# Linear attention and a gated feed-forward block on one core: the operand sums of a Strassen product and the loads of v are moved in the program

## The chip, the cores and the metric

The kernel runs on one core of a Trainium2 chip. The metric is the time of one execution on the device in microseconds (us), the median of several runs. A profiled execution gives the rows that are shown here. The engines are TensorE (PE, with its weight loads as PEld), VectorE (DVE), ScalarE (ACT) and GpSimd (POOL); SyncE (SP) issues most of the DMAs. Each engine works through its own queue in the order of the program; semaphores make it wait for others.

## What is computed

```python
q, k, v: (8, 8, 576, 64)       # batch, heads, sequence, head size; float32
w_gate, w_val: (512, 1536);  w_out: (1536, 512)

q_s = softmax of q over the head size
k_s = softmax of k over the sequence
kv  = einsum('bhsd,bhse->bhde', k_s, v)
x   = einsum('bhsd,bhde->bhse', q_s, kv)   as (4608, 512)
g   = x @ w_gate
out = (gelu(g) * (x @ w_val)) @ w_out      # (4608, 512), gelu with erf
```

## The kernel before

**Blocks.** Tokens are worked on in nine blocks of 512, in the order 0 to 6, 8, 7. Blocks 0 to 7 hold 512 of the 576 tokens of a batch each; block 8 holds the remaining 64 of every batch (called "rem" in the code, `xtr` for its x). `b` is the block, `B` is 8.

**A block's feed-forward part.** The hidden size of 1536 is cut into twelve tiles of 128 (`fi` 0 to 11, "tile 0" to "tile 11" in the text). For each tile TensorE makes `psg` and `psv` by four matmuls of 512 columns each (`mm_gv`, L424). ACT takes GELU of `psg` to `gl` (L429), and VectorE multiplies `psv`, a constant and `gl` to `ht` in float16 (L430; the text calls this the gate). So a gate sets `psv`'s bank free.

**PSUM banks.** Six banks go round in a ring (`ring`, `big`): each new tile takes the bank at the head, and its tag goes to the end at once, or, with `hold=True`, when `let_go` is called. Two more banks (`ps_att`) serve the attention part. A matmul into a bank waits until the bank's former content has been read.

**The output product.** In block 0, h @ w_out is made directly (`mm_out`). In all other blocks `out_strassen` makes it with seven half-size products in place of eight (Strassen and Winograd): h is cut into four quarters (by hidden half and token half), w_out into four, and `product(i, ...)` runs 12 matmuls of 256 columns (L545). For it, VectorE makes four sums of quarters of w_out once (`sum_w`, the tiles `tw`, L514, in block 1), and in each block four sums of quarters of h (`sum_h`, L531): sum 1 and 2 give `sh` 1 and 2, sum 3 overwrites a quarter of `ht`, sum 4 gives `s4`. A sum over hidden tiles j0 to j1 needs the gates of tiles j0 to j1 and 6 + j0 to 6 + j1, so it can be made in parts while the tiles are being finished. Products 1, 2 and 4 read plain `ht`; 5 and 6 read `sh` 1 and 2, 3 reads `s4`, 7 the overwritten quarter. Three banks are held: `psa` (products 1, then 6, 7 and 4 added to it), `psc` (5, then 3 added) and `psb` (2). `snap` copies a bank between two products for the output (`sn`, L571), `add` adds a bank to such a copy and writes `yo` (L577). Products run in the order 1, 5, 6, 3, 7, 2, 4.

**The attention part rides along.** `plan` is a table written by hand: `at(b, FI, i, ...)` puts work behind tile i of block b, `at(b, NS, i, ...)` behind certain products of `out_strassen`; `ride` issues it. For the next batches there are: loads of q, k and v (`load_batch`, issued by SP); exp on ACT (L178); the sums for the softmax of q on VectorE (`norm_sum`, L196, L198) and the multiplication by them on POOL (`norm_mul`, L215); a transpose by DMA (`unit_td`, L343); the cast of v to float16 on POOL (`cast_v`, L154); k's product with v and its normalization (`unit_kv4`, L300); and x by `unit_x4` (L387), with copies to `xt` on ACT and VectorE. There is one buffer for the loaded v (`vt`), and there are two each for q and k.

**Start.** Before block 0, two k sums (`ksum_mm`, `pks`) are made by matmul and inverted on VectorE (`ksum_rec`, `rck`, L270); then k's product with v for four pairs of heads (`kv0_mm`, `pskv`, L278), with the casts of v, x of batch 0, and the first tiles' matmuls.

These lines say where the sums and v's casts stand:

```python
    SUMS = {7: (0, 2), 9: (2, 4), 10: (4, 5)}     # behind these tiles, sums 1 to 4 of these hidden tiles
    for i in range(4):
        at(1, FI, 3 + i, L(sum_w, i + 1))
            at(b, FI, 0, L(load_batch, b + 2))
            at(b, FI, NFI - 1, L(exp, "q", b + 2), L(exp, "k", b + 2), L(cast_v, b + 2, 0, H))
            sum_h(NO - 1, NO, (1, 2))             # after tile 11; sums 3 and 4 of it in out_strassen
```

Of the kernel before, what the change touches and what calls it, by code (L numbers as in the profile page):

```python
# [18 lines left out]
def kernel(  # L19
# [15 lines left out]
    P = 128  # L35
# [39 lines left out]
    def let_go(t):  # L75
        ring.append(held.pop(id(t))[1])
# [183 lines left out]
    def ksum_mm(g):  # L260
        st[("pks", g)] = big([P, 2], f32, "pks")
        for j in range(2):
            hp = 2 * g + j
            for n in range(NC):
                nc.tensor.matmul(st[("pks", g)][:, j:j + 1], ek_b[0][:, n, hp * P:(hp + 1) * P],
                                 ones, start=(n == 0), stop=(n == NC - 1))

    def ksum_rec(g):
        st[("rck0", g)] = att.tile([P, 2], f32, name="rck0", tag="rck0")
        nc.vector.reciprocal(out=st[("rck0", g)], in_=st[("pks", g)])  # L270

    def kv0_mm(hp):
# [259 lines left out]

    SUMS = {7: (0, 2), 9: (2, 4), 10: (4, 5)}

# [14 lines left out]
    def out_strassen(b, last):  # L549
# [25 lines left out]
        def add(nm, sn, half, col):  # L575
            for t, src in parts(nm):
                nc.vector.scalar_tensor_tensor(  # L577
                    out=yo[half][:, t, c[col]], in0=src, scalar=1.0 / _H_SCALE,
                    in1=sn[:, t], op0=ALU.mult, op1=ALU.add)
# [13 lines left out]
        for x in tiles_["c"]:  # L593
            let_go(x)
        product(7, ps["a"], False)
# [115 lines left out]
    def at(b, kind, i, *fns):  # L711
# [30 lines left out]
    at(1, FI, 11, L(load_batch, 3), L(exp, "k", 2, 4, 8), L(exp, "q", 3), L(exp, "k", 3), L(exp_rem0), L(cast_v, 3, 0, H))  # L742
    for i in range(4):
        at(1, FI, 3 + i, L(sum_w, i + 1))
    at(1, FI, 6, make_s)
    at(1, NS, 2, L(unit_kv4, 2))
# [3 lines left out]
    for b in range(2, B):  # L750
        if b + 2 < B:
            at(b, FI, 0, L(load_batch, b + 2))
            at(b, FI, NFI - 1, L(exp, "q", b + 2), L(exp, "k", b + 2), L(cast_v, b + 2, 0, H))
        if b + 1 < B:
            n = b + 1
            for hp in range(HP):
                at(b, FI, hp, L(norm_sum, n, hp), L(norm_mul, n, hp, "pool"))
            at(b, FI, 4, L(unit_td, n))
            if n == 3:
                at(b, FI, 5, L(unit_kv4, n))  # L760
            at(b, NS, 4, L(unit_x4, n, ("act", "dve"), 0 if n == 4 else None))
            if n + 1 < B:
                at(b, NS, 4, L(unit_kv4, n + 1, n == 4))
# [6 lines left out]
    for b in order:  # L770
# [9 lines left out]
        for fi in range(fi0, NFI):  # L780
            ffn_fi(xt, fi, b == 1 and fi == 7)
            ride(b, FI, fi)
            if b > 0 and fi in SUMS:
                sum_h(*SUMS[fi], (1, 2, 3, 4))
        if b == 0:
# [12 lines left out]
        else:  # L798
            sum_h(NO - 1, NO, (1, 2))
            out_strassen(b, b == order[-1])  # L800
# [30 lines left out]
```

## Time and profile before

| | |
|---|---|
| median of 3 runs | 317.51 us (316.55 to 319.07) |
| profiled execution | 317.21 us, its span 315.4 us |
| TensorE matmuls busy | 297.0 us (94%), 2077 of them |
| VectorE busy | 210.7 us (67%), 424 instructions |
| ACT busy | 146.0 us (46%) |
| POOL busy | 78.2 us (25%) |
| mean granted TensorE clock | 0.989 |

How to read the rows: those of the list of waits name the engine, the line and what it waited for, then the total in us, the number of times and the longest. Rows of the timeline give the start in us from the start of the span, the duration, the engine, the line, the operation, its output and inputs with their shapes, and how many of them were joined (x12); in brackets stands the idle time before it and what ended it. Joined matmuls overlap, so a row's duration goes a little beyond the start of the next. Rows of stretches give the stretch, its length, each engine's busy time and count, the granted clock, and the DMAs' share and rate; where TensorE's matmuls alone were asked for, only their busy time stands there. Lines are those of the kernel before.

### The profile page before, as it was taken

How to read it: one execution, taken by the hardware profiler on the slowest of the kernel's cores; microseconds unless marked ns; L12 is line 12 of the kernel's file. 1: busy time of each engine (PE TensorE's matmuls, PEld its weight loads, DVE VectorE, ACT ScalarE, POOL GpSimd, SP SyncE). 2: the span in 40 equal slices, each digit the busy share in tenths (PEclk: the TensorE clock that was granted, in tenths of full speed). 3: DMA queues.
4: the chain of work that ended last, by engine and by line, in shares of the span. 5: the costliest groups of instructions: out<-in, count | busy, mean ns of one | idle time of the engine just before them, and what ended most of it. 6: DMA issues, size and time to landing. Idle time of an engine off the chain costs nothing.

```text
span 315.4 us, 5395 instructions
## 1 busy us (share of the span) xinstructions
PE 297.0 (94%) x2077; PEld 167.9 (53%) x2077; DVE 210.7 (67%) x424; ACT 146.0 (46%) x195; POOL 78.2 (25%) x83
## 2 busy tenths in 40 slices
PE   3899999994999979999999999999999999999994
PEld 1444454442854467446744674458446744674473
DVE  2944386599757885869676957696569535843673
ACT  4753574984573383438343745373532233213320
POOL 2667441075036400540043204410330000000000
PEclk9999999996999999999999999999999999999999
DMA  7999999506959601990099009900340030023003
GB/s 230 372 383 395 400 386 388 148 0 139 383 172 379 131 0 77 355 245 0 25 346 291 9 14 345 310 0 2 133 84 2 11 124 0 0 51 84 1 3 133
DMA packets 54762, 51.67 MB, mean 164 GB/s; under 512 B 18512, under 2 KB 50768, under 8 KB 54736
## 3 DMA queue, kind: packets, MB, share of 16 engines
q1 hardware_dynamic: 53152, 49.75, 49.1%
q10 hardware_dynamic: 1584, 1.57, 1.6%
q8 instruction: 16, 0.26, 0.3%
q14 instruction: 10, 0.08, 0.1%
HBM read 37.75 MB, written 9.44 MB: 150 GB/s over the span
## 4 chain that ended last, share of the span: by engine, by line
PE 79%; DVE 15%; issue 2%; DMA 2%; ACT 1%; DVEq 0%; ACTq 0%
PE psv L424 26%; PE psg L424 25%; PE psa L545 12%; PE psc L545 5%; DVE sh L531 5%; DVE ht L430 4%; PE psb L545 4%; PE psy L492 3%; DMA qt<-in_q_dram 2%; DVE s L531 1%; PE pskv L300 1%; PE psx L387 1%; DVE sn L571 1%; DVE rq L206 1%; PE psx L366 0%
## 5 line engine op out<-in xcount | busy, mean ns | idle before, releaser
L430 DVE SCALAR_TENSOR_TENSOR ht<-psv,gl 128x512 f16<-128x512 f32 x108 | 73.1, 682 | 63.7 <-PE psv L424 47.0
L429 ACT ACTIVATE gl<-psg 128x512 f32<-128x512 f32 x108 | 63.2, 597 | 100.6 <-PE psg L424 93.8
L424 PE MATMUL psv<-xt,wv_sb 128*128 128x512 f16 x384 | 101.4, 382 | 4.5 <-DVE ht L430 4.5
L424 PE MATMUL psg<-xt,wg_sb 128*128 128x512 f16 x384 | 100.6, 379 | 0.0
L424 PEld LDWEIGHTS <-wv_sb 128*128 128x128 f16 x432 | 42.3, 98 | 55.8 <-issue 5.7
L424 PEld LDWEIGHTS <-wg_sb 128*128 128x128 f16 x432 | 42.1, 98 | 48.7
L215 POOL TENSOR_TENSOR eq<-eq,rrq 128x640 f16<-128x640 f16 (+1 forms) x27 | 36.7, 1360 | 112.8 <-DVE rrq L198 80.1
L545 PEld LDWEIGHTS <-ht 128*128 128x128 f16 x384 | 37.6, 99 | 7.8 <-issue 1.4
L154 POOL CAST v<-vt 128x640 f16<-128x640 f32 x26 | 20.5, 826 | 30.0 <-DMA vt<-in_v_dram 30.0
L196 DVE TENSOR_REDUCE rq<-eq 128x10 f32<-128x640 f16 x28 | 22.7, 810 | 4.2 <-ACT eq L178 4.2
L545 PE MATMUL psa<-tw,ht 128*128 128x256 f16 x192 | 23.6, 273 | 0.0
L545 PEld LDWEIGHTS <-sh 128*128 128x128 f16 x192 | 18.7, 98 | 7.3 <-issue 2.7
L178 ACT ACTIVATE ek<-kt 128x1280 f16<-128x1280 f32 (+1 forms) x11 | 19.1, 1748 | 3.7 <-DMA kt<-in_k_dram 3.7
L178 ACT ACTIVATE eq<-qt 128x2560 f16<-128x2560 f32 (+2 forms) x10 | 18.5, 1864 | 4.8 <-DMA qt<-in_q_dram 4.7
L614 ACT ACTIVATE yo<-psa 128x512 f32<-128x512 f32 (+1 forms) x8 | 4.6, 570 | 26.6 <-PE psa L545 26.6
L545 PE MATMUL psc<-tw,sh 128*128 128x256 f16 x96 | 12.6, 276 | 1.4 <-DVE sh L531 1.4
L531 DVE TENSOR_TENSOR sh<-ht 128x512 f16<-128x512 f16 (+1 forms) x32 | 13.1, 411 | 1.1
L531 DVE TENSOR_TENSOR sh<-sh,ht 128x512 f16<-128x512 f16 (+1 forms) x32 | 13.1, 410 | 1.1
L571 DVE TENSOR_SCALAR sn<-psa 128x512 f32<-128x512 f32 (+1 forms) x16 | 10.5, 654 | 4.9 <-PE psa L545 4.9
L545 PE MATMUL psa<-tw,sh 128*128 128x256 f16 x96 | 11.8, 272 | 2.0 <-DVE sn L571 2.0
L545 PE MATMUL psa<-wo_sb,ht 128*128 128x256 f16 x96 | 13.1, 291 | 0.0
L531 DVE TENSOR_TENSOR s<-ht,sh 128x512 f16<-128x512 f16 (+1 forms) x32 | 12.8, 399 | 0.0
(86 smaller groups left out, 258.9 us busy)
## 6 DMA issues: line engine op xcount, KB each, us to landing
out_dram<-yo SPq DMA_DIRECT2D x15, 512.0 KB, 3.0
kt<-in_k_dram SPq DMA_DIRECT2D x7, 640.0 KB, 7.0
vt<-in_v_dram SPq DMA_DIRECT2D x7, 640.0 KB, 8.6
qt<-in_q_dram SPq DMA_DIRECT2D x7, 640.0 KB, 5.5
qt<-in_q_dram SPq DMA_DIRECT2D x8, 512.0 KB, 6.2
wost<-in_moe_w_out_dram SPq DMA_DIRECT2D x6, 512.0 KB, 7.9
kt<-in_k_dram SPq DMA_DIRECT2D x6, 512.0 KB, 7.5
vt<-in_v_dram SPq DMA_DIRECT2D x6, 512.0 KB, 9.1
```

The costliest lines, as they stand in the source:

```text
L154: nc.gpsimd.tensor_copy(out=dst, in_=src)
L178: nc.scalar.activation(out=dst[:, n0:NC, h0 * D:h1 * D].rearrange(o, d=D, **({"t": 2} if b >= QUAD else {})), in_=heads(tiles[(nm, b)], b, ...
L196: nc.vector.reduce_sum(rq, e, axis=mybir.AxisListType.X)
L215: (nc.gpsimd if eng == "pool" else nc.vector).tensor_tensor(out=e, in0=e, in1=rrq.unsqueeze(-1).to_broadcast((P, n, 2, D)), op=ALU.mult)
L424: nc.tensor.matmul(ps, w[:, ci, fi * P:(fi + 1) * P], xt[:, ci, :], start=(ci == 0), stop=(ci == HP - 1))
L429: nc.scalar.activation(out=gl, in_=psg, func=ACTF.Gelu)
L430: nc.vector.scalar_tensor_tensor(out=ht[:, fi, :], in0=psv, scalar=_H_SCALE, in1=gl, op0=ALU.mult, op1=ALU.mult)
L492: nc.tensor.matmul(psy, ht[:, fi, ns * P:(ns + 1) * P], wo_sb[:, fi, :], start=(fi == 0), stop=(fi == NFI - 1))
L531: nc.vector.tensor_tensor(out=o, in0=a, in1=b, op=op)
L545: nc.tensor.matmul(ps[t], a, w, start=(first and j == 0 and (t == ts[0] or ps[t].tensor is not ps[ts[0]].tensor)), stop=(j == NO - 1), ski ...
L571: nc.vector.tensor_scalar(out=sn[:, t], in0=src, scalar1=1.0 / _H_SCALE, scalar2=None, op0=ALU.mult)
L614: nc.scalar.activation(out=yo[1][:, t, c[0]], in_=src, func=ACTF.Copy, scale=1.0 / _H_SCALE)
```

## The change

It has five parts.

1. Two sums of w_out move to VectorE's queue among the first three tiles of block 1, two behind tile 3.
2. The sums of h are made in twos: 1 and 2 behind tiles 7 and 9, 3 and 4 behind tiles 8 and 10, and the last third in one piece over two hidden tiles around the end of tile 11.
3. Product 2, of plain h, runs second, right behind product 1, in blocks 1 to 6; in blocks 8 and 7 ("late") it keeps its place.
4. From block 2 on, v is loaded ahead of q and k, and its casts are written behind tile 4, after the multiplications of q.
5. A k sum holds its bank until it has been inverted.

VectorE in block 1, from the normalization of k's product with v (`kv_sb`) to the fourth tile of the part that alternates gates and softmax sums, before:

```order
L253 SCALAR_TENSOR_TENSOR kv_sb<-pskv,rck,mask 128x128 x2
L158 CAST xt<-psx 128x512
L430 SCALAR_TENSOR_TENSOR ht<-psv,gl 128x512 x4
L196 TENSOR_REDUCE rq<-eq_87 128x10
L198 RECIPROCAL rrq<-rq 128x10
L514 TENSOR_TENSOR tw_738<-wo_sb 128x1536
L430 SCALAR_TENSOR_TENSOR ht<-psv,gl 128x512
L196 TENSOR_REDUCE rq<-eq_87 128x10
L198 RECIPROCAL rrq<-rq 128x10
L514 TENSOR_TENSOR tw_758<-wo_sb,tw_738 128x1536
```

The same stretch of VectorE's queue in the changed kernel:

```order
L253 SCALAR_TENSOR_TENSOR kv_sb<-pskv,rck,mask 128x128 x2
L515 TENSOR_TENSOR tw_687<-wo_sb 128x1536
L158 CAST xt<-psx 128x512
L515 TENSOR_TENSOR tw_698<-wo_sb,tw_687 128x1536
L431 SCALAR_TENSOR_TENSOR ht<-psv,gl 128x512 x4
L515 TENSOR_TENSOR tw_736<-wo_sb 128x1536
L515 TENSOR_TENSOR tw_738<-wo_sb,tw_698 128x1536
L196 TENSOR_REDUCE rq<-eq_87 128x10
L198 RECIPROCAL rrq<-rq 128x10
L431 SCALAR_TENSOR_TENSOR ht<-psv,gl 128x512
```

All four sums (`tw`) now stand ahead of the first softmax sum (`rq`), and none between the later ones.

VectorE from the gate of tile 7 to the copies for the output, in a block from 2 to 5, before (four gates, twelve sums until tile 11, then four narrow ones):

```order
L531 TENSOR_TENSOR sh_800<-ht 128x512
L531 TENSOR_TENSOR sh_801<-sh_800,ht 128x512
L531 TENSOR_TENSOR ht<-ht 128x2x256
L531 TENSOR_TENSOR s_94<-ht,sh_801 128x512
L430 SCALAR_TENSOR_TENSOR ht<-psv,gl 128x512 x2
...
L430 SCALAR_TENSOR_TENSOR ht<-psv,gl 128x512
L531 TENSOR_TENSOR sh_800<-ht 128x256
L531 TENSOR_TENSOR sh_801<-sh_800,ht 128x256
L571 TENSOR_SCALAR sn<-psa 128x512
L531 TENSOR_TENSOR ht<-ht 128x256
L531 TENSOR_TENSOR s_94<-ht,sh_801 128x256
L571 TENSOR_SCALAR sn<-psc 128x512
```

And in the changed kernel:

```order
L532 TENSOR_TENSOR sh_764<-ht 128x512
L532 TENSOR_TENSOR sh_765<-sh_764,ht 128x512
L431 SCALAR_TENSOR_TENSOR ht<-psv,gl 128x512
L532 TENSOR_TENSOR ht<-ht 128x2x256
L532 TENSOR_TENSOR s_94<-ht,sh_765 128x512
...
L532 TENSOR_TENSOR sh_764<-ht 128x512
L532 TENSOR_TENSOR sh_765<-sh_764,ht 128x512
L572 TENSOR_SCALAR sn<-psa 128x512
L578 SCALAR_TENSOR_TENSOR yo<-psb,sn 128x2x256
L532 TENSOR_TENSOR s_94<-ht,sh_765 128x512
L532 TENSOR_TENSOR ht<-ht 128x2x256
L572 TENSOR_SCALAR sn<-psc 128x512
```

A gate now stands between sums 2 and 3, and the sum of `psb` behind the first copy of `psa`; it stood behind the copies of x before.

SP's queue of DMAs at the start of a block from 2 on, the stores of the block before (`yo`) first, before:

```order
L502 DMA out_dram<-yo 64x2x1024 x2
L134 DMA qt_100<-in_q_dram 64x8x320
L134 DMA qt_100<-in_q_dram 64x8x256
L134 DMA kt_97<-in_k_dram 64x8x320
L134 DMA kt_97<-in_k_dram 64x8x256
L134 DMA vt_99<-in_v_dram 64x8x320
L134 DMA vt_99<-in_v_dram 64x8x256
L343 DMA_TRANSPOSE eqt<-eq_90 128x20x128
```

And in the changed kernel:

```order
L503 DMA out_dram<-yo 64x2x1024 x2
L134 DMA vt_99<-in_v_dram 64x8x320
L134 DMA vt_99<-in_v_dram 64x8x256
L134 DMA qt_100<-in_q_dram 64x8x320
L134 DMA qt_100<-in_q_dram 64x8x256
L134 DMA kt_97<-in_k_dram 64x8x320
L134 DMA kt_97<-in_k_dram 64x8x256
L344 DMA_TRANSPOSE eqt<-eq_90 128x20x128
```

The two DMAs of v stand first; the order on POOL and ACT is what it was.

The core of the diff:

```diff
     def ksum_mm(g):
-        st[("pks", g)] = big([P, 2], f32, "pks")
+        st[("pks", g)] = big([P, 2], f32, "pks", True)
...
         nc.vector.reciprocal(out=st[("rck0", g)], in_=st[("pks", g)])
+        let_go(st[("pks", g)])
...
-    SUMS = {7: (0, 2), 9: (2, 4), 10: (4, 5)}
+    SUMS = {7: (0, 2, (1, 2)), 8: (0, 2, (3, 4)), 9: (2, 4, (1, 2)), 10: (2, 4, (3, 4))}
...
+        def second():
+            get("b")
+            product(2, ps["b"], True)
+            add("b", s1, 0, 0)
+            for x in tiles_["b"]:
+                let_go(x)
+
+        late = b == B or last
         get("a")
         product(1, ps["a"], True)
         s1 = snap("a")
-        sum_h(NO - 1, NO, (3, 4))
+        if not late:
+            second()
+        sum_h(NO - 2, NO, (4,))
         get("c")
         product(5, ps["c"], True)
+        if not late:
+            sum_h(NO - 2, NO, (3,))
         s5 = snap("c")
+        if late:
+            sum_h(NO - 2, NO, (3,))
...
-        get("b")
-        product(2, ps["b"], True)
-        add("b", s1, 0, 0)
-        store_rows(b, 0, yo[0])
-        for x in tiles_["b"]:
-            let_go(x)
+        if late:
+            second()
+            store_rows(b, 0, yo[0])
...
-    first1 = [[L(unit_t, 1, 1), L(unit_kv, 1, 1)], [L(unit_x, 1, 2, "act")],
-              [L(unit_x, 1, 3, "dve")]]
+    first1 = [[L(unit_t, 1, 1), L(unit_kv, 1, 1)], [L(unit_x, 1, 2, "act"), L(sum_w, 1)],
+              [L(unit_x, 1, 3, "dve"), L(sum_w, 2)]]
...
-    at(1, FI, 3, L(exp, "q", 2), L(norm, 2, 0, "pool"))
+    at(1, FI, 3, L(sum_w, 3), L(sum_w, 4), L(exp, "q", 2), L(norm, 2, 0, "pool"))
...
-            at(b, FI, 0, L(load_batch, b + 2))
-            at(b, FI, NFI - 1, L(exp, "q", b + 2), L(exp, "k", b + 2), L(cast_v, b + 2, 0, H))
+            at(b, FI, 0, L(load_batch, b + 2, ((v, "v"), (q, "q"), (k, "k"))))
+            at(b, FI, NFI - 1, L(exp, "q", b + 2), L(exp, "k", b + 2))
+            vcast = L(cast_v, b + 2, 0, H)
...
+            if n + 1 < B:
+                at(b, FI, 4, vcast)
...
-                sum_h(*SUMS[fi], (1, 2, 3, 4))
+                sum_h(*SUMS[fi])
...
-            sum_h(NO - 1, NO, (1, 2))
+            sum_h(NO - 2, NO, (1, 2))
```

More of the change, by code (lines that the diff above doesn't have):

```diff
@@ L594, in out_strassen @@
             let_go(x)
+        if not late:
+            store_rows(b, 0, yo[0])
         product(7, ps["a"], False)
@@ L600, in out_strassen @@
                 store(nc.sync, yo[1][:, t, c[1]], b, 2 + t, 3 + t, 256, 512)
-        get("b")
-        product(2, ps["b"], True)
-        add("b", s1, 0, 0)
-        store_rows(b, 0, yo[0])
-        for x in tiles_["b"]:
-            let_go(x)
+        if late:
+            second()
+            store_rows(b, 0, yo[0])
         for ts in ((0,), (1,)) if last else ((0, 1),):
@@ L742 @@
     at(1, FI, 11, L(load_batch, 3), L(exp, "k", 2, 4, 8), L(exp, "q", 3), L(exp, "k", 3), L(exp_rem0), L(cast_v, 3, 0, H))
-    for i in range(4):
-        at(1, FI, 3 + i, L(sum_w, i + 1))
-    at(1, FI, 6, make_s)
+    at(1, FI, 4, make_s)
     at(1, NS, 2, L(unit_kv4, 2))
```

## Prediction

> **What bounds the kernel now.** I read the page first: the clock and the chain that ended last.
>
> ```profile
> PEclk9999999996999999999999999999999999999999
> PE 79%; DVE 15%; issue 2%; DMA 2%; ACT 1%; DVEq 0%; ACTq 0%
> ```
>
> TensorE sets the end; VectorE holds 15% of the chain, so something on it makes TensorE wait. One slice of forty has a low clock. The list of waits names the places:
>
> ```profile
> PE psv L424 <- DVE ht L430: 4.5, 1, 4.5
> PE psa L545 <- DVE sn L571: 2.0, 4, 0.5
> PE psc L545 <- DVE sh L531: 1.4, 2, 1.1
> ```
>
> The first is one stall, in block 1. The other two recur where the output products begin. To size them I took the stretch from the first matmul of product 1 to the first of product 6 (two products of 12 matmuls) in blocks 2, 3, 4, 5 and 6:
>
> ```profile
> 111.25:115.87 4.62, 2.95 (x24) 1.00 0.00 0
> 144.62:148.12 3.50, 2.96 (x25) 1.00 0.00 0
> 176.99:180.17 3.18, 2.78 (x24) 1.00 0.00 0
> 208.91:212.66 3.75, 2.96 (x24) 1.00 0.00 0
> 241.41:244.07 2.66, 2.66 (x25) 1.00 0.00 0
> ```
>
> The first figure is the length in us. Block 6 has no casts of v, and loses nothing: 2.66. The others lose 1.96, 0.84, 0.52 and 1.09 against it, 4.41 together. This is the most that blocks 2 to 5 can win here.
>
> **Blocks 2 to 5: sums in twos, plain product second, early casts.** Block 5 from tile 7 on (start, duration; tile 7's gate, the casts, sums, last gate; the last multiply of the normalization; the casts of x and the product behind them). First stand the issue of q, and the time from issue to landing of such loads when they are the first of three:
>
> ```profile
> 189.66 1.48 SPq L134 DMA_DIRECT2D qt<-in_q_dram  x2
> ...
> qt<-in_q_dram SPq DMA_DIRECT2D x7, 640.0 KB, 5.5
> ...
> 197.91 1.26 POOL L215 TENSOR_TENSOR eq<-eq,rrq 128x640 f16<-128x640 f16 x1 [0.36 <-DVE rrq L198]
> 202.28 0.69 DVE L430 SCALAR_TENSOR_TENSOR ht<-psv,gl 128x512 f16<-128x512 f32 x1 [1.03 <-PE psv L424]
> 202.75 3.28 POOL L154 CAST v<-vt 128x640 f16<-128x640 f32 x4 [3.59 <-DMA vt<-in_v_dram]
> 204.52 0.93 DVE L531 TENSOR_TENSOR ht<-ht 128x512 f16<-128x512 f16 x1
> 207.54 0.42 DVE L531 TENSOR_TENSOR sh<-ht 128x512 f16<-128x512 f16 x1
> 208.05 1.03 PE L424 MATMUL psv<-xt,wv_sb 128*128 128x512 f16 x4
> 209.01 0.68 DVE L430 SCALAR_TENSOR_TENSOR ht<-psv,gl 128x512 f16<-128x512 f32 x1
> 210.67 0.68 DVE L430 SCALAR_TENSOR_TENSOR ht<-psv,gl 128x512 f16<-128x512 f32 x1
> 217.60 1.28 DVE L158 CAST xt<-psx 128x512 f16<-128x512 f32 x2
> 219.38 1.48 PE L545 MATMUL psa<-tw,ht 128*128 128x256 f16 x12
> ```
>
> A sum beside POOL's casts takes 0.93, and 0.42 without them. Four sums without them occupy 207.54 to 209.01, so two cost about 0.75. POOL is free at 197.91 + 1.26 = 199.17, but waits 3.59 for v. Loaded first, v takes q's place: issued until 191.1, landed 5.5 later, near 196.6 (between that and 202.3, where it lands as third, 199.2 is the limit; I take the nearer row, q's). Then the casts follow the multiplies directly; unhindered they need less than the 3.28, and end near 202.2, ahead of the first sums at 203.0. Beside them VectorE has only gates, which read PSUM and took 0.69 at 202.28 as at 209.01.
>
> I then set VectorE's queue by hand, with these durations. TensorE's tiles come every 1.73 (eight matmuls, 1.03 for an overlapped four); a gate (0.7) and two sums (0.75) fit, so each gate starts when its psv is done. Tile 11's: 208.05 + 1.03 + 0.1 = 209.2, done 209.9, instead of 210.67. The last pair of sums ends at 210.65, the snapshot of psa at 211.35. TensorE does product 1 until 210.22, product 2 until 211.53, product 5 until 212.84. Product 2's last operand is ready 1.4 before it is read, and product 6's snapshot 1.5 before. What product 2 puts into VectorE's queue, the sum of psb (0.69, as the same operation on psa below), comes after that snapshot, and the snapshot of psc behind it ends at 213.8, with product 3 due at 214.15: the tightest place, 0.3. No wait remains: **4.41 saved**. Should the casts stay where they are, four sums at 0.93 delay VectorE by some 1.8, and product 2 covers 1.3 of it; 0.5 in each of four blocks would come back.
>
> Product 2 used to stand between x and the next block's first tile. Now only product 4 does: its end moves from 220.69 to 219.37 on this scale, while the casts of x end at 217.60 + 1.28 = 218.88. Cover 0.5; each us above that costs 4 over four blocks. Block 6 has no matmuls for k and v there, and pays:
>
> ```profile
> 248.20 0.69 DVE L577 SCALAR_TENSOR_TENSOR yo<-psa,sn 128x512 f32<-128x512 f32 x1 [0.62 <-PE psa L545]
> 248.71 1.48 PE L545 MATMUL psb<-wo_sb,ht 128*128 128x256 f16 x12
> ```
>
> Product 4 takes psb's place at 248.71, and must wait until psa is read at 248.89: **0.2 lost** (0.24 with the semaphore).
>
> The new SP order makes k land last, near 202.3 on this scale; ACT takes it only behind tile 11's GELU, not before 209. In blocks 8 and 7 the order of products stays; without product 2 in between, the snapshot of psa (211.35) is still 0.2 ahead of product 6 (211.53). Neither counts. The narrower last sums before (256 wide, eight a block) become four of 512: VectorE's queue gets 24 instructions shorter, which is in the hand schedule already.
>
> **Block 1.** Its rows, in order of time:
>
> ```profile
> 53.88 0.69 DVE L158 CAST xt<-psx 128x512 f16<-128x512 f32 x1 [1.32 <-PE psx L366]
> 56.02 1.89 DVE L430 SCALAR_TENSOR_TENSOR ht<-psv,gl 128x512 f16<-128x512 f32 x3 [1.45 <-PE psv L424]
> 61.61 0.82 DVE L196 TENSOR_REDUCE rq<-eq 128x10 f32<-128x640 f16 x1 [2.65 <-ACT eq L178]
> 65.15 0.96 DVE L514 TENSOR_TENSOR tw<-wo_sb,tw 128x1536 f16<-128x1536 f16 x1
> 66.03 0.68 DVE L430 SCALAR_TENSOR_TENSOR ht<-psv,gl 128x512 f16<-128x512 f32 x1
> 70.37 1.77 POOL L215 TENSOR_TENSOR eq<-eq,rrq 128x640 f16<-128x640 f16 x1 [0.63 <-PE psv L424]
> 72.17 3.08 SPq L343 DMA_TRANSPOSE eqt<-eq  x1
> 75.64 1.87 PE L424 MATMUL psv<-xt,wv_sb 128*128 128x512 f16 x4 [4.47 <-DVE ht L430]
> 81.69 2.34 ACT L178 ACTIVATE eq<-qt 128x2560 f16<-128x2560 f32 x1 [2.83 <-DMA qt<-in_q_dram]
> 84.83 2.34 ACT L178 ACTIVATE ek<-kt 128x2560 f16<-128x2560 f32 x1 [0.80 <-DMA kt<-in_k_dram]
> 88.00 1.06 ACT L156 CAST xt<-psx 128x512 f16<-128x512 f32 x2
> 89.67 1.03 PE L424 MATMUL psg<-xt,wg_sb 128*128 128x512 f16 x4
> 75.60:80.40 4.80, 4.76 (x19) 2.72 (x19) 4.59 (x13) 3.15 (x3) 0.00 (x0) 0.51 0.93 250
> ```
>
> Before, the sums of w_out (0.96 each) stand between the normalization's steps, and TensorE stalls 4.47 for the gate that frees psv; then it runs 4.8 at a clock of 0.51 (last row), which costs another 2.35. The new places are idle time: 1.32, 1.45 and, for the last two, 2.65. So all four cost nothing there; without that cover, 0.9 each.
>
> How far does TensorE come? The gate that frees psv ended just before psv started, at 75.6. Three sums of w_out (0.87 each from start to start, 65.15 to 66.03) leave the queue ahead of it, the first being hidden behind a GELU anyway, and the two later sums of h (0.87 each beside POOL) now follow it: 75.6 - 2.6 - 1.7 = 71.3, where psv is due at 71.0. Tile 11's gate follows after a pair of sums at 1.7, two at 0.75 and three gates at 0.7: 76.4. Product 2's last pair waits for it. Then come products 5, 6, 3 and 7 (1.31 each), the matmuls of k and v and of x (1.5) and product 4 with its wait: TensorE would be ready for block 2 at 84.9. But **what is late next is a load**. ACT's casts of x stand behind exp of batch 3's q and k, which waited 2.83 and 0.80 for their DMAs; SP issues those right behind the transpose at 72.17, and that behind POOL's last multiply. Of the sums of w_out, two count for that multiply (the fourth stood behind its reciprocal): 2 x 0.87 = 1.74. And POOL's multiply, no longer beside a sum, takes 1.26 as in block 5 or a bit more, not 1.77: 2.05 together. The casts end at 89.06 - 2.05 = 87.01. The second group of matmuls of block 2 needs the second cast, so its start counts as 86.83: **2.84 saved**. Bounds: 2.0 if POOL's multiplies stay long, 4.8 if TensorE alone decides.
>
> **K sums that hold their bank.**
>
> ```profile
> 14.54 0.38 PE L366 MATMUL psx<-eqt,kv_sb 128*128 128x512 f16 x1
> 14.96 0.58 ACT L156 CAST xt<-psx 128x512 f16<-128x512 f32 x1 [0.18 <-PE psx L366]
> 15.76 0.35 PE L278 MATMUL pskv<-v,ek 128*64 128x64 f16 x10 [0.84 <-DVE rck L270]
> ```
>
> The third pskv gets the bank of the second k sum, and waits for its reciprocal. Holding it gives pskv another bank; it can start 0.3 behind psx, at 14.85. The next tile then waits for the cast that ends at 15.54. I take **0.85**; bounds 0 (weights or block 0's loads decide later) and 0.91.
>
> **Sum.** 0.85 + 2.84 + 4.41 - 0.24 = 7.86. The profiled execution took 317.21 (span 315.4), the median of the runs is 0.3 above it. 317.21 - 7.86 = 309.35; I say 309.4.
>
> **Rivals.**
> 1. *The half clock stays.* TensorE would still stand about 1.7 before block 2, with 0.65 and 1.06 in product 2 shortly before. If that again drops the clock for 4.8, it costs 2.35: 311.7. Against it: block 2's stretch above lost 1.96, and its clock is 1.00. For it: the clock fell inside a stall of 4.47. [...] Chance 0.2.
> 2. *Block 1 gives nothing:* batch 3's loads land when they did, since DMA and not the transpose sets them; ACT's casts stay, and TensorE waits longer. 309.4 + 2.8 = 312.2. For it the waits of 2.83 and 0.80; against it SP's issue directly behind 72.17. Chance 0.1.
> 3. *The casts do not leave the sums,* since v lands no earlier than POOL's turn plus 3: 0.5 in four blocks, 311.4. The change would then not do what it says. Chance 0.08.
> 4. *Slower:* product 2 now reads tile 11's h right behind product 1. If VectorE is more than 1.4 late, TensorE stands in every block; late by as much as in block 1, each of blocks 2 to 5 pays what block 1 pays now, 4.47 + 2.35. It decides from two blocks: 309.4 + 13.6 = 323.0. Against it: the margin of 1.4. Chance 0.04.
>
> **How the numbers follow.** Forecast 0.55; the remaining 0.03 is for anything else. Upper bounds of the savings (0.91, 4.8, 4.41, no loss in block 6) give 307.1; the half clock with no gain from the held bank gives 312.6. The runs of before lie from 1.0 below to 1.6 above their median, so I add half a us above. Range 307.0 to 313.2; it leaves out rival 4 and little more. A measurement here tells about 1% from no change, so faster means below 314.3: the forecast and rivals 1 to 3, less a little, 0.9; same 0.06; slower 0.04.
>
> **What would show it.** No wait of psv for ht in block 1 above 1 us; the clock 1.00 there; the transpose near 69.3; ACT's second exp still ended by a DMA. Sums at 0.42 in blocks 2 to 5, POOL's casts ended before them; stretch from product 1 to product 6 at 3.97 (three products). A start of pskv near 14.9. Wrong it would be by a wait at product 2's last pair, a late xt in blocks 2 to 5, or v landing after tile 7.

## The result and the profile after

| | before | changed |
|---|---|---|
| median of four runs, us | 317.03 (316.24 to 319.07) | 309.25 (308.66 to 310.83) |
| profiled execution, us | 317.21, span 315.4 | 310.83, span 309.0 |
| mean granted clock in it | 0.989 | 0.994 |

The ratio is 0.975, 95% interval 0.969 to 0.980: faster, by 7.8 us where 7.9 was forecast (317.21 to 309.35 in the prediction's sum). The profiled execution of the changed kernel is the longest of its four; why it is 1.5 above the next is part of what follows. The changed file is one line longer above most functions, so L430 of before is L431 now, L531 is L532, L545 is L546.

The page, clock and chain of the changed kernel:

```profile
PEclk9999999999979999999999999999999999999999
PE 89%; DMA 5%; POOL 1%; SPq 1%; ACT 1%; DVE 1%; issue 1%; POOLq 0%; ACTq 0%
```

VectorE's share of the chain went from 15% to 1%, and a chain of other engines took a part of its place: POOL, SP's queue, DMA, ACT. The list of what TensorE waits for, without the warm-up and the start:

```profile
PE psg L425 <- ACT xt L156: 1.9, 1, 1.9
PE psb L546 <- DVE ht L431: 0.9, 1, 0.9
PE psv L425 <- DVE ht L431: 0.5, 1, 0.5
...
PE psa L546 <- DVE yo L578: 0.2, 1, 0.2
```

Four single waits, 3.5 us together: psv's and psb's are in block 1, psg's is ahead of block 2's first tile, and psa's is in block 6. The 4.5 for psv is 0.5. Blocks 2 to 5 wait for nothing, as the stretch from the first matmul of product 1 to the first of product 6 shows (three products now, 1.31 each; blocks 2 to 6):

```profile
109.28:113.21 3.93, 3.93 (x38) 3.53 (x36) 3.60 (x9) 3.92 (x3) 0.00 (x0) 1.00 0.00 0
140.64:144.57 3.93, 3.93 (x37) 3.52 (x36) 3.25 (x7) 3.92 (x3) 0.00 (x0) 1.00 0.00 0
172.14:176.07 3.93, 3.93 (x37) 3.51 (x36) 3.25 (x7) 3.92 (x3) 0.00 (x0) 1.00 0.00 0
203.51:207.44 3.93, 3.93 (x37) 3.53 (x36) 3.25 (x7) 3.92 (x3) 0.00 (x0) 1.00 0.00 0
234.88:238.81 3.93, 3.93 (x37) 3.53 (x36) 3.25 (x7) 0.00 (x0) 0.00 (x0) 1.00 0.01 2
```

Block 5 in the timeline of the changed kernel (GpSimd's casts of v, the first sum of h, tile 11's gate; VectorE's casts of x; then, in block 6, product 4 with its wait):

```profile
193.70 2.72 POOL L154 CAST v<-vt 128x640 f16<-128x640 f32 x4
...
197.60 0.42 DVE L532 TENSOR_TENSOR sh<-ht 128x512 f16<-128x512 f16 x1
...
203.78 0.69 DVE L431 SCALAR_TENSOR_TENSOR ht<-psv,gl 128x512 f16<-128x512 f32 x1 [0.37 <-PE psv L425]
...
212.38 1.28 DVE L158 CAST xt<-psx 128x512 f16<-128x512 f32 x2
...
243.69 1.47 PE L546 MATMUL psa<-tw,ht 128*128 128x256 f16 x12 [0.16 <-DVE yo L578]
```

The casts end at 196.4, before the first sum starts at 197.6, and sums take 0.42. VectorE waits for psv ahead of the last gate: it has time again. Its casts of x end at 213.7, half a us before product 4 does, as worked out. Block 1 and the start of block 2, in order of time (the third product of k and v at the start; a sum of w_out; GpSimd's last multiply and the sum of h beside it; the transpose; the two waits; ACT's two exp of batch 3; block 2's first group):

```profile
14.81 0.35 PE L279 MATMUL pskv<-v,ek 128*64 128x64 f16 x10
...
57.88 0.95 DVE L515 TENSOR_TENSOR tw<-wo_sb 128x1536 f16<-128x1536 f16 x1
...
67.52 1.26 POOL L215 TENSOR_TENSOR eq<-eq,rrq 128x640 f16<-128x640 f16 x1 [0.32 <-PE psv L425]
...
67.94 1.12 DVE L532 TENSOR_TENSOR sh<-ht 128x512 f16<-128x512 f16 x1
...
68.80 3.08 SPq L344 DMA_TRANSPOSE eqt<-eq  x1
...
70.56 1.02 PE L425 MATMUL psv<-xt,wv_sb 128*128 128x512 f16 x4 [0.45 <-DVE ht L431]
...
75.15 0.39 PE L546 MATMUL psb<-wo_sb,ht 128*128 128x256 f16 x2 [0.88 <-DVE ht L431]
...
78.39 2.34 ACT L178 ACTIVATE eq<-qt 128x2560 f16<-128x2560 f32 x1 [4.60 <-DMA qt<-in_q_dram]
...
81.95 2.34 ACT L178 ACTIVATE ek<-kt 128x2560 f16<-128x2560 f32 x1 [1.22 <-DMA kt<-in_k_dram]
...
85.75 1.29 PE L425 MATMUL psg<-xt,wg_sb 128*128 128x512 f16 x4 [1.86 <-ACT xt L156]
```

The clock right behind it, from the table by stretches (the number after the engines' times):

```profile
87.25:90.50 3.25, 3.25 (x10) 1.11 (x8) 1.42 (x2) 1.96 (x3) 0.96 (x2) 0.50 0.59 182
```

Block 2 starts at 85.75 instead of 89.67, and ACT's exp still wait for DMA. Behind the wait of 1.86 the clock is 0.50 for 3.4 us, which costs 1.7. It is the digit 7 in the clock row of the page, and it accounts for the 1.5 by which this execution is longer than the next.

### The profile page after: what moved, and what is told of

Same layout as the page of the kernel before. It is cut to its first block, busy times and chain, and to the rows that moved or that the text cites. A ratio compares the mean times of both kernels' runs of the same rounds, so it can differ in the third digit from the quotient of the medians.

```text
span 309.0 us, 5369 instructions
## 1 busy us (share of the span) xinstructions
PE 295.9 (96%) x2077; PEld 167.6 (54%) x2077; DVE 204.1 (66%) x392; ACT 146.0 (47%) x195; POOL 74.3 (24%) x83
## 4 chain that ended last, share of the span: by engine, by line
PE 89%; DMA 5%; POOL 1%; SPq 1%; ACT 1%; DVE 1%; issue 1%; POOLq 0%; ACTq 0%
PE psg L425 30%; PE psv L425 30%; PE psa L546 12%; PE psc L546 6%; PE psy L493 3%; PE psb L546 3%; DMA vt<-in_v_dram 3%; DMA qt<-in_q_dram 2%; PE pskv L301 1%; SPq L134 1%; POOL v L154 1%; PE pst L326 1%; PE psx L388 1%; PE psx L367 1%; POOL eq L215 1%
## 5 line engine op out<-in xcount | busy, mean ns | idle before, releaser
L431 DVE SCALAR_TENSOR_TENSOR ht<-psv,gl 128x512 f16<-128x512 f32 x108 | 73.7, 685 | 67.6 <-PE psv L425 49.1
L430 ACT ACTIVATE gl<-psg 128x512 f32<-128x512 f32 x108 | 63.3, 598 | 98.1 <-PE psg L425 96.5
L215 POOL TENSOR_TENSOR eq<-eq,rrq 128x640 f16<-128x640 f16 (+1 forms) x27 | 34.4, 1276 | 125.6 <-issue 92.3
L546 PEld LDWEIGHTS <-ht 128*128 128x128 f16 x384 | 37.1, 98 | 8.6 <-DVE ht L431 1.5
L546 PE MATMUL psa<-tw,ht 128*128 128x256 f16 x192 | 23.6, 273 | 0.2 <-DVE yo L578 0.2
L154 POOL CAST v<-vt 128x640 f16<-128x640 f32 x26 | 18.5, 754 | 14.7 <-DMA vt<-in_v_dram 14.7
L546 PEld LDWEIGHTS <-sh 128*128 128x128 f16 x192 | 18.8, 98 | 2.2
L546 PE MATMUL psb<-wo_sb,ht 128*128 128x256 f16 x96 | 12.1, 273 | 1.0 <-DVE ht L431 0.9
L425 PE MATMUL psg<-xtr,wg_sb 128*128 128x512 f16 x48 | 12.3, 379 | 0.0
L425 PE MATMUL psv<-xtr,wv_sb 128*128 128x512 f16 x48 | 12.3, 379 | 0.0
L546 PE MATMUL psc<-wo_sb,s 128*128 128x256 f16 x96 | 11.8, 273 | 0.0
L546 PE MATMUL psa<-tw,sh 128*128 128x256 f16 x96 | 11.8, 273 | 0.0
L546 PE MATMUL psa<-wo_sb,ht 128*128 128x256 f16 x96 | 11.8, 273 | 0.0
```

The lines of the kernel that those rows point to most:

```text
L154: nc.gpsimd.tensor_copy(out=dst, in_=src)
L215: (nc.gpsimd if eng == "pool" else nc.vector).tensor_tensor(out=e, in0=e, in1=rrq.unsqueeze(-1).to_broadcast((P, n, 2, D)), op=ALU.mult)
L425: nc.tensor.matmul(ps, w[:, ci, fi * P:(fi + 1) * P], xt[:, ci, :], start=(ci == 0), stop=(ci == HP - 1))
L430: nc.scalar.activation(out=gl, in_=psg, func=ACTF.Gelu)
L431: nc.vector.scalar_tensor_tensor(out=ht[:, fi, :], in0=psv, scalar=_H_SCALE, in1=gl, op0=ALU.mult, op1=ALU.mult)
L546: nc.tensor.matmul(ps[t], a, w, start=(first and j == 0 and (t == ts[0] or ps[t].tensor is not ps[ts[0]].tensor)), stop=(j == NO - 1), ski ...
```

## The experiments

In each, TensorE's rows of blocks 2 to 5 give the loss of a block: the time from the first matmul of product 1 to the first of product 6, less 1.31 for each product that runs in it. By this measure the four blocks lost 4.57 before; the prediction measured against block 6's 2.66, which holds 0.04 of its own, and so had 4.41. Losses behind product 6 are named where there are any. Medians of four comparisons stand side by side below. The kernel before had 316.76 to 317.31 in three of them and 318.61 in one, so differences of half a us rest on the traces.

### The changed kernel again

> The changed kernel again, as the measure for the three beside it. Expected as before: about 309.2 where the clock stays full, about 310.8 where it is halved once behind the wait ahead of block 2 (there the first profile shows TensorE standing 2.02 and then one stretch of 3.4 us at half clock). In blocks 2 to 5 TensorE has no wait; the only real wait of block 1 is the one ahead of block 2, for batch 3's k.

308.41 (308.35 to 308.98), ratio 0.972 [0.969, 0.974]. The exp of k and block 2's start in this profile, whose span is 306.6:

```profile
81.17 2.34 ACT L178 ACTIVATE ek<-kt 128x2560 f16<-128x2560 f32 x1 [0.57 <-DMA kt<-in_k_dram]
...
84.97 1.29 PE L425 MATMUL psg<-xt,wg_sb 128*128 128x512 f16 x4 [1.14 <-ACT xt L156]
```

k landed 0.8 earlier than in the first profile, block 2 started 0.8 earlier, and the clock stayed full behind the wait. Why k landed earlier is open: the transpose ahead of its load was issued within 0.1 of the same time. So two things vary from run to run here: when batch 3's k lands, and whether the wait behind it costs half clock.

### One of the three edits to blocks 2 to 5 undone

v loaded last again:

```diff
-            at(b, FI, 0, L(load_batch, b + 2, ((v, "v"), (q, "q"), (k, "k"))))
+            at(b, FI, 0, L(load_batch, b + 2))
```

> The changed kernel, but with q, k, v loaded in the old order in blocks 2 to 5 (the casts of v stand in the same place of GpSimd's queue either way, so the load order is what decides). Theory: v lands about 3 us later, the casts run beside the sums again (0.93 instead of 0.42 each, VectorE up to 1.8 late), the plain product in second place covers 1.3 to 1.4 of it: 0.4 to 0.5 lost in each of four blocks, 1.6 to 2.0 in all, about 311. Rival 1, the cover is enough: 0 to 0.3 in all. Rival 2, without the early load all is lost: 4.4, about 313.6. In the trace: a cast of v beside tile 7 or later, sums of 0.9 there, and a wait at product 2's last pair or none.

309.36 (308.84 to 309.67), ratio 0.974 [0.971, 0.977]. In block 3 of its timeline the casts stand beside the sums (the second row is one of two long ones), and the last gate follows:

```profile
133.00 3.37 POOL L154 CAST v<-vt 128x640 f16<-128x640 f32 x4 [4.12 <-DMA vt<-in_v_dram]
...
134.85 0.93 DVE L532 TENSOR_TENSOR s<-ht,sh 128x512 f16<-128x512 f16 x1
...
138.90 0.69 DVE L431 SCALAR_TENSOR_TENSOR ht<-psv,gl 128x512 f16<-128x512 f32 x1 [0.32 <-PE psv L425]
```

v lands late and sums are long, as expected; but VectorE has caught up by the last gate, where it waits 0.32 for TensorE. Blocks 3 to 5 lose nothing. Block 2 loses 0.5 at product 3, behind the measured stretch; the list of waits counts 0.3 of it, for the snapshot of psc:

```profile
PE psc L546 <- DVE sn L572: 0.3, 1, 0.3
```

My 0.5 in each of four blocks was wrong in three of them; rival 1 (0 to 0.3) is nearer in the trace. The two profiled executions differ by just this 0.5; the rest of the 0.95 between the medians has no wait of its own.

Product 2 behind product 7 again:

```diff
-        late = b == B or last
+        late = True
```

> The changed kernel, but with the product of plain h (product 2) behind product 7 in every block, as it was before. Theory: the short sums alone (0.42, casts of v out of the way, two sums per tile) already bring VectorE in time: by the rows of block 2 the sums of the last tiles end at 111.2 while product 5 would read them at 111.6, and the snapshot of psa ends at 111.83 while product 6 would begin at 112.06. So blocks 2 to 5 lose nothing, block 6 wins its 0.24 back, and block 1, where product 5 would wait about 2.0 instead of product 2's 1.3, hides that under its wait for the load: 0 to -0.3 in all. Rival: the cover of product 2 is what carries the gain; then 0.5 to 1.1 comes back in each of four blocks as waits for sums or snapshots, 2 to 4.4 in all.

308.48 (308.15 to 309.54), ratio 0.972 [0.969, 0.975]: no change. Its waits, without the start:

```profile
PE psc L546 <- DVE sh L532: 1.8, 1, 1.8
PE psv L425 <- DVE ht L431: 0.5, 1, 0.5
PE psa L546 <- DVE sn L572: 0.4, 1, 0.4
```

All three are in block 1. Psv's stands in the changed kernel too; the other two stand in place of product 2's 0.9, and no wait for the load stands ahead of block 2: they take its time. Blocks 2 to 5 lose 0.00, and block 6 no longer waits. The theory holds.

The sums of h in the old groups:

```diff
-    SUMS = {7: (0, 2, (1, 2)), 8: (0, 2, (3, 4)), 9: (2, 4, (1, 2)), 10: (2, 4, (3, 4))}
+    SUMS = {7: (0, 2, (1, 2, 3, 4)), 9: (2, 4, (1, 2, 3, 4)), 10: (4, 5, (1, 2, 3, 4))}
...
-            sum_h(NO - 2, NO, (1, 2))
+            sum_h(NO - 1, NO, (1, 2))
```

> The changed kernel, but with the sums of h in the old groups: four behind tile 7, four behind tile 9, four narrow ones behind tile 10 and the rest in the last stretch. Theory: a gate (0.7) and four sums (1.5) exceed a tile (1.73) by 0.45, which the next tile gives back; the last gate comes about 0.75 later than now, product 2's last pair has a margin of 1.4, so blocks 2 to 5 lose 0 to 0.3 each. In block 1 the wait of psv for a gate grows from 0.5 to about 2, hidden under the wait for batch 3's loads: 0 to 1.2 in all. Rival: the twos carry the gain; a wait at product 2 or product 5 of 0.5 or more in each of four blocks, 2 or more in all.

308.92 (308.74 to 309.08), ratio 0.973 [0.970, 0.976]. Blocks 2 to 5 lose 0.00. In block 1 psv waits (timeline) and the clock halves (stretches):

```profile
72.46 1.87 PE L425 MATMUL psv<-xt,wv_sb 128*128 128x512 f16 x4 [2.17 <-DVE ht L431]
```

```profile
72.50:75.30 2.80, 2.80 (x10) 1.35 (x10) 2.70 (x7) 2.77 (x3) 0.00 (x0) 0.50 0.88 176
```

Block 2 starts at 85.90, 0.9 later than in the changed kernel beside it, though TensorE lost 2.2 plus 1.7 here. Two losses of the changed kernel are gone in return, 1.3 each from start to start: product 2's last pair no longer waits for its gate, nor block 2 for the load. So none of the three edits alone carries the gain of blocks 2 to 5. Each can go, and the other two keep it, but for the 0.5 in block 2 without v's early load.

### One of the three edits alone

> The changed kernel with only v's early load kept of the three edits to blocks 2 to 5: the sums of h in the old groups, and product 2 behind product 7. Theory, the casts beside the sums are the whole cause: without them the old groups of sums are in time, as in block 6 of the kernel before (stretch from product 1 to product 6 of 2.66); 0 to 0.1 in blocks 3 to 5, up to 0.5 in block 2, where VectorE has the normalization of block 0's q as well. Block 1 has its psv wait of about 2.3 with the half clock, as with the old sums alone, and the stretch to block 2 hides most of it. 308.5 to 310. Rival, twos or order carry it: 0.5 to 1 in each of four blocks, 310.5 to 312.5.

> The changed kernel with only product 2's early place kept of the three: v third in the loads, the sums of h in the old groups. Theory, a delay that one product of 1.31 covers: before, blocks 2 to 5 lost 1.96, 0.84, 0.52 and 1.09; less 1.31 each, 0.65 is left in block 2 and up to 0.3 in the others, where product 2 itself waits for tile 11's gate; 0.7 to 1.5 in all over the changed kernel, plus block 1 as with the old sums alone: 309.5 to 310.5. Rival, the cover does not reach, since product 2 reads what the late gate writes: 3 to 4.4 in all, 312 or more.

> The changed kernel with only the sums in twos kept of the three: v third in the loads, product 2 behind product 7. Theory, from the run with v's old load alone: there two to three sums in a block are long (0.8 to 0.93), and in blocks 3 to 5 VectorE has caught up by the last gate; the sum that product 5 reads is ready 0.7 before it would be read. So blocks 3 to 5 lose 0 to 0.1 each, and block 2 about 1.2 (0.4 at product 5, 0.6 at product 6, the rest at product 3). 309.4 to 310. Rival: each block loses 0.5 to 1, 311 to 312.

| kept of the three | us, median | ratio to before | loss in block 2 | 3 | 4 | 5 |
|---|---|---|---|---|---|---|
| none (the kernel before) | 316.76 | 1 | 2.00 | 0.88 | 0.56 | 1.13 |
| v loaded first | 310.21 | 0.980 [0.977, 0.983] | 0.79 | 0.04 | 0.04 | 0.04 |
| product 2 early | 310.14 | 0.979 [0.977, 0.981] | 1.19 | 0.00 | 0.00 | 0.01 |
| sums in twos | 309.70 | 0.978 [0.975, 0.980] | 1.43 | 0.00 | 0.00 | 0.00 |
| all three | 308.41 | 0.972 [0.969, 0.974] | 0.00 | 0.00 | 0.00 | 0.00 |

(The before of the first four is that of their own comparison, its losses are those of the first profile; the last row is from the comparison above. All rows but the first have the change's parts for the start and for block 1. Each of these kernels is faster than before; for those with one edit the intervals leave open whether by 2%.) In blocks 3 to 5 any one of the three wins nearly all of the 2.57 that was lost there; with product 2 alone, 0.2 more is lost behind the stretch, at product 3, in each of blocks 2 and 5. Only block 2 needs more than one.

No run has none of the three beside the change's other parts, which could have helped blocks 3 to 5 by themselves. With product 2 alone, VectorE's snapshot of psa in block 3 shows how late it still is:

```profile
142.15 0.68 DVE L572 TENSOR_SCALAR sn<-psa 128x512 f32<-128x512 f32 x1
```

It ends 2.99 behind product 1's start at 139.84, and 2.99 and 3.60 behind it in blocks 4 and 5. In the old order product 6 would read psa after 2.62. By these rows some 1.7 of the 2.57 would still be lost without the cover; the other parts can have won 0.9 at most (an estimate).

The waits of block 2, with the sums alone, and with product 2 alone:

```profile
110.05 0.61 PE L546 MATMUL psc<-tw,sh 128*128 128x256 f16 x4 [0.64 <-DVE sh L532]
...
111.11 1.47 PE L546 MATMUL psa<-tw,sh 128*128 128x256 f16 x12 [0.45 <-DVE sn L572]
```

```profile
110.68 0.39 PE L546 MATMUL psb<-wo_sb,ht 128*128 128x256 f16 x2 [1.01 <-DVE ht L431]
```

With the sums alone the expectation (1.2 in block 2, 0 to 0.1 elsewhere) nearly holds. With product 2 alone block 2 keeps more than the 0.65 expected: its last pair waits for the late gate, which is the mechanism of the rival, in this one block. v's load alone was expected to leave 0 to 0.5 in block 2 and left 0.79, most of it ahead of product 6, which waits for the snapshot of psa.

### Why block 2: the normalization of block 0's q

Made from the kernel with the sums alone:

```diff
-    at(2, FI, 7, L(norm_rem0))
+    at(2, FI, 5, L(norm_rem0))
```

> The kernel with only the sums in twos kept of the three edits to blocks 2 to 5, which lost 1.42 in block 2 (0.81 at product 5 and 0.61 at product 6) and nothing in blocks 3 to 5; here the normalization of block 0's q (three operations of VectorE, 0.67, 0.20 and 1.20 in that run) stands behind tile 5 of block 2 instead of tile 7, where VectorE waits 1.0 to 1.3 per tile anyway. Theory, block 2 differs from the others by these operations alone: its two waits go, 1.3 to 1.4 less than the run it is made from, about 308.3. Rival, block 2 differs by what is left over from block 1 (late loads, a late v): both waits stay, 309.7.

The loss of block 2 went from 1.43 to 0.00, the other blocks stay at 0.00. 309.17 (308.57 to 309.26), ratio 0.972 [0.967, 0.977], against 0.978 without the edit; the runs of before spread from 316.25 to 318.94 there, so the size rests on the trace. The last of the three operations, before the edit and after it (both kernels' timelines, block 2):

```profile
101.96 1.20 DVE L232 TENSOR_TENSOR eq0r<-eq0r,rrq 64x512 f16<-64x512 f16 x1
```

```profile
98.52 0.69 DVE L232 TENSOR_TENSOR eq0r<-eq0r,rrq 64x512 f16<-64x512 f16 x1
```

Behind tile 7 it ran beside the casts (1.20), and the three operations pushed the first sums back by 2.0; behind tile 5 they fill time in which VectorE waited anyway. What is left over from block 1 is not the difference: in both runs VectorE waits 0.42 for psv ahead of tile 5's gate, and the casts start 0.8 to 0.9 behind the start of tile 7's gate. So these three operations made block 2 the worst with the sums alone. In the kernel before they stand in the same place, ahead of the late sums; that they explain its 2.00 as well is likely, and was not run.

### The sums of w_out at their old places

```diff
-    first1 = [..., [L(unit_x, 1, 2, "act"), L(sum_w, 1)], [L(unit_x, 1, 3, "dve"), L(sum_w, 2)]]
+    first1 = [..., [L(unit_x, 1, 2, "act")], [L(unit_x, 1, 3, "dve")]]
-    at(1, FI, 3, L(sum_w, 3), L(sum_w, 4), ...)
+    at(1, FI, 3, ...)
-    at(1, FI, 4, make_s)
+    for i in range(4):
+        at(1, FI, 3 + i, L(sum_w, i + 1))
+    at(1, FI, 6, make_s)
```

(`make_s` allots the buffers of `sh` 1 and 2 and goes back with them.)

> The changed kernel, but with the four sums of w_out at their old places, behind tiles 3 to 6 of block 1. Theory: they stand again between the normalization's steps, so that GpSimd's last multiply, and with it the transpose and batch 3's loads, come 2.0 to 2.4 later, and VectorE's gate that frees psv as well; block 2 starts 2.0 to 2.4 later: 310.4 to 311 at full clock, up to 312.7 where the clock is halved behind a wait of psv of 2.5 to 3. Rival, the sums in twos and product 2 absorb it as they did in blocks 2 to 5: 308.5 to 309. In the trace: a wait of psv for a gate near 2.8, the transpose near 71.

311.23 (311.13 to 311.38), ratio 0.981 [0.979, 0.984]: 2.8 more than the changed kernel. Transpose, psv's wait and block 2's start:

```profile
71.09 3.03 SPq L344 DMA_TRANSPOSE eqt<-eq  x1
```

```profile
72.85 1.54 PE L425 MATMUL psv<-xt,wv_sb 128*128 128x512 f16 x4 [2.77 <-DVE ht L431]
...
87.74 1.29 PE L425 MATMUL psg<-xt,wg_sb 128*128 128x512 f16 x4 [1.22 <-ACT xt L156]
```

The transpose is 2.35 later than the 68.74 of the changed kernel's second profile, block 2 2.77 later. TensorE lost 2.8 and another 1.7 at half clock (from start to start psv's four matmuls took 1.34 instead of 0.86, product 1 2.50 instead of 1.31), and still waits 1.22 for ACT behind all that. Since a wait for the load is left even so, the stall is not what the old places cost: the chain from GpSimd's multiply over the transpose and the loads is. The theory holds, the rival falls.

### The loads themselves moved

Batch 3's q and k issued at tile 4 of block 1, ahead of the transpose:

```diff
-    at(1, FI, 11, L(load_batch, 3), L(exp, "k", 2, 4, 8), ...)
-    at(1, FI, 4, make_s)
+    at(1, FI, 11, L(load_batch, 3, ((v, "v"),)), L(exp, "k", 2, 4, 8), ...)
+    at(1, FI, 4, make_s, L(load_batch, 3, ((q, "q"), (k, "k"))))
```

> The changed kernel with batch 3's q and k loaded from tile 4 of block 1 on instead of behind the transpose at tile 11 (v stays there, its buffer is not free before). Theory, the load sets block 2's start: the two exp follow the last exp of batch 2 directly, the casts of x stand at 83 or before, and the wait of 1.1 to 2.0 ahead of block 2 goes: 1.3 to 2.3 less than the changed kernel, 306.1 to 307.2, and no half clock behind block 1. Next would be VectorE's casts of x, 0.3. Rival 1, the wait stays since ACT's or VectorE's casts of x are late anyway: 308.4. Rival 2, the loads delay batch 2's transfers or the stores that run beside them: 308.4 or more.

306.95 (306.90 to 307.08), ratio 0.969 [0.967, 0.971], clock 1.00 in every run. ACT's exp of batch 3's q and block 2's first group:

```profile
73.76 2.32 ACT L178 ACTIVATE eq<-qt 128x2560 f16<-128x2560 f32 x1
```

```profile
83.80 1.03 PE L425 MATMUL psg<-xt,wg_sb 128*128 128x512 f16 x4
```

The exp waits for nothing, the wait ahead of block 2 is gone, and the runs lie within 0.2 of each other. This shows that the load set block 2's start. That its landing and the clock behind it made the changed kernel's runs differ fits too: nothing of either is left here.

### The k sums not holding their bank

```diff
-        st[("pks", g)] = big([P, 2], f32, "pks", True)
+        st[("pks", g)] = big([P, 2], f32, "pks")
...
-        let_go(st[("pks", g)])
```

> The changed kernel, but with the two k sums not holding their banks. Theory: the third pskv waits for the reciprocal again and everything behind starts 0.8 to 0.95 later: 309.2 to 309.4 against 308.4. Rival, the start's loss is absorbed by the wait for batch 3's loads ahead of block 2 or by later weight loads: 308.4. In the trace: the third pskv near 15.75 instead of 14.8, and block 1's start 0.9 to 1.0 later.

309.77 (309.34 to 309.83), ratio 0.976 [0.974, 0.979].

```profile
16.02 0.35 PE L278 MATMUL pskv<-v,ek 128*64 128x64 f16 x10 [0.84 <-DVE rck L270]
```

The wait of 0.84 is back (this file is one line shorter, so the line is L278 again). Measured from the psx ahead of it, pskv starts 1.22 behind instead of 0.31, so 0.91 of the 1.36 between the medians is this bank. Block 1 starts at 49.83, 1.25 later than in the changed kernel's second profile, and 0.36 of that was there before psx. Nothing later absorbed the loss: block 2 starts at 86.37, 1.4 later.

### A faster version

The earlier loads, and batch 2's v cast ahead of GpSimd's multiplies, and product 2 late in block 6 too:

```diff
-        late = b == B or last
+        late = b >= B - 2
...
-    at(1, FI, 3, L(sum_w, 3), L(sum_w, 4), L(exp, "q", 2), L(norm, 2, 0, "pool"))
+    at(1, FI, 3, L(sum_w, 3), L(sum_w, 4), L(cast_v, 2, 0, H), L(exp, "q", 2), L(norm, 2, 0, "pool"))
-    at(1, FI, 7, L(exp, "k", 2, 0, 4), L(cast_v, 2, 0, H))
+    at(1, FI, 7, L(exp, "k", 2, 0, 4))
```

> The changed kernel with three edits: batch 3's q and k loaded from tile 4 of block 1 on; the casts of batch 2's v ahead of GpSimd's multiplies instead of behind them, so that no sum of h in block 1 runs beside them; product 2 behind product 7 in block 6. Theory: v2 lands near 57.5, the casts run until about 61.5, in GpSimd's idle time; they slow two sums of w_out, which costs VectorE time that it waits in anyway; the first sums of h take 0.42 instead of 1.12, 0.82 and 0.93, which takes most of the waits of 0.6 and 1.3 in block 1 away, and block 6 wins 0.2: 305.0 to 305.8, against 306.95 with the earlier loads alone. Rival 1: the casts wait for v2 until 58 or more and push GpSimd's multiplies back by 1 to 2, and with them VectorE waits for nothing, but the transpose comes later and block 2 waits for x: 306.7 to 308. Rival 2: the slowed sums of w_out delay the normalization by 0.8 and give back half: 306.2.

305.73 (305.65 to 305.87), ratio 0.964 [0.961, 0.967]: the fastest here. The casts of v, the sum of w_out beside them, a sum of h, and what TensorE still waits for:

```profile
58.24 3.86 POOL L154 CAST v<-vt 128x640 f16<-128x640 f32 x4 [9.43 <-PE psg L425]
```

```profile
58.71 1.47 DVE L515 TENSOR_TENSOR tw<-wo_sb,tw 128x1536 f16<-128x1536 f16 x1
...
69.03 0.42 DVE L532 TENSOR_TENSOR sh<-sh,ht 128x512 f16<-128x512 f16 x1
```

```profile
74.17 0.39 PE L546 MATMUL psb<-wo_sb,ht 128*128 128x256 f16 x2 [0.64 <-DVE ht L431]
```

One sum of w_out took 0.5 longer, in time that VectorE had; all sums of h but the first are short, psv no longer waits, and block 2 starts at 82.75. It is 1.2 below the earlier loads alone, at the lower end of the 1.2 to 1.9 expected: the first sum of h still takes 1.09 beside GpSimd's last multiply, and product 2's last pair still waits.

## Why the prediction was right, point by point

- **The sum.** Against the profile without the half clock (span 306.57, before 315.43): block 1's start 49.63 to 48.58, 1.05 where 0.85 was forecast; block 1 another 3.65 where 2.84 was; all behind it 4.16 where 4.41 - 0.24 = 4.17 was. Together 8.9 instead of 7.9. In the first profile block 1 gave 2.93 and the half clock took 1.7 back. The medians of the two sets of runs are 309.25 and 308.41; that the first lies within 0.2 of the forecast is partly luck. The term that was mis-sized is block 1's: it moves by 0.7 with the time at which batch 3's k lands, and I had read that time from one execution.
- **Held bank.** pskv at 14.81, forecast 14.85; the run without it shows 0.91.
- **Block 1.** Transpose 68.80 (near 69.3), psv's wait 0.45 (below 1), ACT's exp still ended by a DMA: each as forecast. Product 2 lost 1.3 from start to start, 0.88 of it in the list of waits, where 0.65 and 1.06 were put, and the wait ahead of block 2 was 1.86 and 1.14, where about 1.7 was. GpSimd's multiplies fell to 1.26 as assumed, and the run with the old places shows 2.8 for this part alone.
- **"The clock 1.00 there"**: right inside block 1, not behind it. Rival 1, given 0.2, happened in the first profiled run and, by the clocks of the other seven runs of this kernel (0.997 to 1.0), in none of them; its price was 1.7 (one stretch of 3.4), not 2.35. A wait of 1.86 stood ahead of the fall here, one of 4.47 in the kernel before (the other falls stand in the last section).
- **Blocks 2 to 5.** The total was right (0.00 left), its reason only in part. I set the three edits up as a chain in which the casts had to leave and product 2 had to cover ("Should the casts stay where they are, four sums at 0.93 delay VectorE by some 1.8, and product 2 covers 1.3 of it; 0.5 in each of four blocks would come back."). That step failed: with the casts back, two of the four sums were long and not all, and blocks 3 to 5 lost nothing, nor did they with product 2 behind product 7 as well. Before, the lateness in these three was 0.6 to 1.1, and each edit alone covers nearly all of it; I priced each as if the others were needed. Block 2's loss has a reason that I did not name, the three operations of block 0's q.
- **Block 6.** Product 4 waits for the read of psa at 243.69, by 0.23 over an ordinary step; forecast 0.24. With product 2 behind product 7 it is gone.
- **Rivals 2, 3 and 4.** The loads did follow the transpose (2 falls). The casts did leave (196.4; 3 falls). Product 2's last pair waits in block 1 alone (4 falls).

## What to carry to other kernels

Where several edits aim at one wait, size the lateness block by block and ask of each edit alone whether it covers it: three were made here, any one would nearly have done in three of four blocks, and the fourth had a cause of its own. Before shortening an engine's stall, follow the chain behind it to the load that ends last: moving that load's issue ahead of a transpose won 1.5 us with two lines, and the runs then agreed to 0.2. A wait also hides what stands before it: in block 1, 2.2 of stall and 1.7 of half clock moved block 2 by 0.9, since two later waits fell away.

## What the runs showed of the hardware

**Half clock after short waits.** Two kernels have the same two waits of TensorE in block 1, the sums alone and the same with block 0's q moved. In the first, timeline and then stretch:

```profile
75.63 0.61 PE L546 MATMUL psc<-tw,sh 128*128 128x256 f16 x4 [1.84 <-DVE sh L532]
```

```profile
77.10:80.20 3.10, 3.10 (x63) 2.63 (x62) 2.09 (x5) 1.68 (x1) 0.00 (x0) 1.00 1.07 385
```

In the second:

```profile
75.54 0.61 PE L546 MATMUL psc<-tw,sh 128*128 128x256 f16 x4 [1.83 <-DVE sh L532]
```

```profile
77.10:80.20 3.10, 3.10 (x51) 2.29 (x50) 1.66 (x5) 1.51 (x1) 0.00 (x0) 0.54 1.06 385
```

Waits of about 1.84 and 0.45 stand in both, and the clock falls in one. So it is with a wait of psv in block 1: 2.17 with the sums in the old groups, 2.17 with v's load alone, 2.16 with product 2 alone; the clock behind it, in 72.5:75.3, is 0.50 in the first and 1.00 in the other two.

Five of the fourteen profiles have a fall ahead of the kernel's last matmuls. The waits before it were 4.47 in the kernel before, 1.86 in the changed kernel's first profile, 2.17 with the old groups, 2.77 with the sums of w_out at their old places, and 1.83 and 0.45 in the second kernel above. The half clock lasted 6.83 in the kernel before (73.51 to 80.34) and 3.41 in the changed kernel (87.18 to 90.59). The stretch of the same length ahead of the latter, with matmuls busy for 1.45 of it:

```profile
83.77:87.18 3.41, 1.45 (x8) 0.57 (x6) 0.56 (x1) 2.96 (x8) 1.70 (x3) 1.00 0.34 135
```

The ends of matmuls are modelled in the records, so the 1.45 is uncertain by some tenths. Waits of some 2 us in all cost 1.7 more in some of these runs and nothing more in others. What decides was not shown. In the traces of the kernel before and of the changed one the changes of the clock stand at multiples of 3.413 us from its first rise: 19, 21 and 90 in the one, 23, 24 and 88 in the other. In the second kernel above, the clocks of its stretches (0.54 in 77.10:80.20, 0.95 in 80.50:83.00) put the fall near 77.35 and the rise near 80.75, 3.4 later; the 3.41 ahead of that fall, 73.94 to 77.35, hold both waits but for the first 0.2. That the place of the waits against such steps decides is an estimate of mine: where the steps lie in the first kernel no row shows, and no run was made to test it.

**Sums and multiplies side by side.** GpSimd's multiply took 1.77 to 1.87 in the kernel before, beside VectorE's sums of w_out, and 1.26 without them; a sum of h took 0.42 alone, 0.79 to 0.94 beside casts, 1.09 to 1.12 beside a multiply. With v loaded last and the sums in twos, two of the four sums behind tiles 7 and 8 were long beside casts in each of blocks 2 to 5, not all four. That left VectorE about 0.9 late instead of the 1.8 that the prediction put, and in blocks 3 to 5 it had caught up by the last gate.
